# Re-planned start and tail of a fused attention and MLP kernel: denser warm-up matmuls, 2 KB weight rows with strided w_in columns, last 256 tokens as weights of the second layer

## The chip, the core and the metric

The kernel runs on one core of one Trainium2 chip. TensorE (PE) multiplies, VectorE (DVE) and ScalarE (ACT) move and transform tiles, GpSimd (POOL) does some of the elementwise products, and SyncE (SP) issues nearly all transfers. The metric is the device time of one execution in microseconds; lower is better. It was run three times before the change, and one more execution was profiled.

## The reference

```python
def phi(x):
    a = np.einsum('rd,bhsd->bhsr', S1, x)
    b = np.einsum('rd,bhsd->bhsr', S2, x)
    return np.einsum('bhsi,bhsj->bhsij', a, b).reshape(*x.shape[:-1], r * r)
q_p, k_p = (phi(q), phi(k))
kv = np.einsum('bhsf,bhsd->bhfd', k_p, v)
z = np.sum(k_p, axis=2)
num = np.einsum('bhsf,bhfd->bhsd', q_p, kv)
den = np.einsum('bhsf,bhf->bhs', q_p, z)[..., None] + 1e-06
attn_out = (num / den).astype(np.float32)
x = np.ascontiguousarray(attn_out.transpose(0, 2, 1, 3)).reshape(B * S, H * D)
h = x @ w_in
g = h - np.tanh(h)
out = (g @ w_out).astype(np.float32)
```

Here q, k and v are 4 batches x 4 heads x 1088 positions x 32, r is 8, x is 4352 tokens x 128, w_in is 128 x 2048 and w_out is 2048 x 128. All inputs and the output are float32.

## The kernel before, in words

The attention is linear: keys and values of a batch are summed into a 64 x 32 matrix per head, and the queries of that batch are multiplied with it. Its result for all four heads is the token matrix `xT` (128 features on the partitions, 4352 tokens along them, bf16). The second half works on `xT` in windows of tokens: two of 256, seven of 512, and a last one of 256 (line 945 to 947).

In a window (`layers`, line 891) the first layer makes 16 blocks of 128 hidden units: for each block `jb` the 128 columns `w_in[:, 128*jb:128*jb+128]` are the weights of a matmul and the window's tokens are its moving operand (L913). ACT takes the tanh of each pair or group of blocks out of PSUM into `tt` (L917). The second layer uses `w_out[:, jb, :]` as weights and `tt` as moving operand, and accumulates 16 blocks in PSUM bank 0 (L926). The linear part h @ w_out is not computed from h. Instead w_in @ w_out is folded once into a 128 x 128 matrix (`linear_turn` L858 transposes w_in, L863 copies it, `linear_product` L870 multiplies), it is split in a high and a low bf16 part, and two matmuls per window (L898) add it to the same accumulator. The accumulator holds output features on the partitions and tokens along them, so DVE transposes it in 32 x 32 blocks into `osb` (L932), and four transfers with runs of 128 bytes write it out (L939). For the last window two of those four go through ACT's queue.

Which token sits in which column of `xT`: position s of a batch is j * 34 + c with j below 32 (partition of a transfer) and c below 34, and `xT` orders tokens by c first and j second. So 32 neighbouring columns are 32 tokens that lie 34 rows apart in the output.

The attention of batch 0 is spread over finer steps than that of batches 1 to 3, because everything waits for it. Its path is: keys in (`load_keys` L466), transposed by DVE (L574), projected by PE (L583), transposed back (L591), Gram matrix (L599), masked (L604), folded (L607), reduced to the denominators' weights (L610); then queries projected (L752), transposed (L760), denominators (L779 to L788), products (L662), turned by PE (L677), copied (L684), multiplied with the key-value matrix (L694), copied to `xT` (L700). Batches 1 to 3 do the same in bigger steps, interleaved with the windows: their numerators are at L821 and their copies into `xT` at L831 and L836.

The start needs some constants. `psk` and `s2blk` are the sketches S1 and S2 laid out for the projections. They come from two PE matmuls on `s_raw` (L536, L552), and a third one on a constant `e4` (L549) makes a head mask, which ACT copies out of PSUM (L555). `kvb` (L531, called from `values_first`) is a block-diagonal copy that is made by multiplying with a mask `pmask`.

PE also runs dummy matmuls on a zero tile `wz` while it waits for the first data (L504 with 512 columns, L505 with 128). They are put in by `Program.schedule` (lines 185 to 201) wherever the planned start of the next real matmul leaves room. Their results are not used.

What sets the order: each operation is an `Op` with an engine, an estimated cost and the tiles it reads and writes. The dictionary `ORDER` (line 37) lists, for each engine, the numbers of its operations in the order in which they are issued. Each engine runs its list strictly in order and waits on semaphores where an operand is not ready. SP's list holds loads and stores together. A load may also be held back until an earlier load has landed (`gated`, with a limit of `AHEAD` bytes). So a changed operation can only start when all that stands before it in its engine's list has started, and the change replaces the whole `ORDER`.

The load of w_out (L493) reads four pieces of 512 rows:

```python
out=w_out_f[:, 4 * x:4 * x + 4, :],
in_=moe_w_out[512 * x:512 * x + 512, :].rearrange("(jb ji) c -> ji jb c", jb=4)
```

Partition ji thus gets four separate rows of 512 bytes. POOL casts each piece to bf16 (L848). Of the four pieces of w_in two are cast by ACT and two by POOL (L844).

Of the kernel before, what the change touches and what calls it, by code (L numbers as in the profile page):

```python
# [30 lines left out]
COLD = 6800  # L31
CHUNK = 256
# [20 lines left out]
    ),  # L53
    "scalar": (
# [4 lines left out]
    ),  # L59
    "vector": (  # L60
# [5 lines left out]
    ),  # L66
# [277 lines left out]
def bass_polysketch_attn__then__act_tanh_shrink_kernel(nc, q, k, v, S1, S2, moe_w_in, moe_w_out, out):  # L344
# [546 lines left out]
    def layers(w, f0, n, widths, hooks):  # L891
# [38 lines left out]
        if not f0:  # L930
            lin()
# [134 lines left out]
```

## Time and profile before

| What | us |
|---|---|
| median of 3 runs | 108.34 (107.26, 108.47, 108.34) |
| the profiled execution's own time | 107.41 |
| span of its profile | 105.6 |
| PE busy / ACT / DVE / POOL | 97.0 / 78.5 / 60.4 / 35.9 |
| 70 tanh on ACT (L917) | 66.9 |
| first first-layer matmul starts | 16.25 |
| last second-layer matmul ends | about 102.0 |

The span is shorter than the execution's time by 1.81 us, which lie outside the profiled instructions. The profile's times start at the span's start. In the listing by time, the first number of a line is the start, the second the length of the merged piece; "PEld" is the weight load of TensorE, which overlaps its matmuls; a bracket names how long the engine had been idle and what ended that.

### The profile page before, as it was taken

How to read it: one execution, taken by the hardware profiler on the slowest of the kernel's cores; microseconds unless marked ns; L12 is line 12 of the kernel's file. 1: busy time of each engine (PE TensorE's matmuls, PEld its weight loads, DVE VectorE, ACT ScalarE, POOL GpSimd, SP SyncE). 2: the span in 40 equal slices, each digit the busy share in tenths (PEclk: the TensorE clock that was granted, in tenths of full speed). 3: DMA queues.
4: the chain of work that ended last, by engine and by line, in shares of the span. 5: the costliest groups of instructions: out<-in, count | busy, mean ns of one | idle time of the engine just before them, and what ended most of it. 6: DMA issues, size and time to landing. Idle time of an engine off the chain costs nothing.

```text
span 105.6 us, 2945 instructions
## 1 busy us (share of the span) xinstructions
PE 97.0 (92%) x1243; PEld 50.2 (48%) x1254; DVE 60.4 (57%) x128; ACT 78.5 (74%) x107; POOL 35.9 (34%) x45
## 2 busy tenths in 40 slices
PE   6899899999999969989899999999999999999960
PEld 2557556774576433423644343544444434345540
DVE  2378966899899999198389546892550020200210
ACT  3340588746768836769899796989969999899930
POOL 5637058710946700884900059176000000000000
PEclk9999999999999999999999999999999999999998
DMA  2999999603841503799202300035013222015263
GB/s 46 288 218 346 321 313 243 239 20 72 261 120 19 151 20 77 189 228 253 73 0 33 51 6 0 6 53 87 0 22 50 46 43 44 0 31 91 36 94 55
DMA packets 26509, 11.21 MB, mean 106 GB/s; under 512 B 19072, under 2 KB 24320, under 8 KB 26496
## 3 DMA queue, kind: packets, MB, share of 16 engines
q1 hardware_dynamic: 25920, 10.95, 42.9%
q8 instruction: 10, 0.16, 0.6%
q10 hardware_dynamic: 576, 0.07, 0.4%
q14 instruction: 3, 0.02, 0.1%
HBM read 8.78 MB, written 2.23 MB: 104 GB/s over the span
## 4 chain that ended last, share of the span: by engine, by line
PE 58%; DMA 12%; DVE 10%; ACT 5%; SPq 4%; POOL 4%; issue 3%; POOLq 0%; DVEq 0%
PE ps L926 21%; PE ps L913 21%; DMA w_out_f<-in_moe_w_out_dram 5%; ACT tt L917 5%; PE ps L821 4%; DMA vx<-in_v_dram 4%; PE ps L898 4%; DMA out_dram<-osb 3%; DVE qpT L804 3%; POOL w_out L848 2%; DVE qp L798 2%; DVE osb L932 2%; SPq L480 2%; PE ps L752 1%; DVE qab L760 1%
## 5 line engine op out<-in xcount | busy, mean ns | idle before, releaser
L917 ACT ACTIVATE tt<-ps 128x1024 bf16<-128x1024 f32 (+1 forms) x70 | 66.9, 998 | 10.9 <-PE ps L913 10.2
L913 PE MATMUL ps<-xT,w_in 128*128 128x512 bf16 (+1 forms) x151 | 40.4, 346 | 1.3 <-issue 0.6
L926 PE MATMUL ps<-tt,w_out 128*128 128x512 bf16 (+1 forms) x158 | 39.7, 347 | 0.2 <-issue 0.2
L630 POOL TENSOR_TENSOR wk<-kab 128x768 f32<-128x768 f32 (+2 forms) x11 | 15.7, 1424 | 22.7 <-DVE kab L591 22.2
L913 PEld LDWEIGHTS ps<-xT,w_in 128*128 128x128 bf16 x160 | 14.0, 97 | 17.5 <-ACT tt L917 5.5
L926 PEld LDWEIGHTS ps<-tt,w_out 128*128 128x128 bf16 x160 | 15.3, 99 | 13.2 <-issue 1.3
L932 DVE STREAM_TRANSPOSE osb<-ps 128x512 f32<-128x512 f32 (+1 forms) x10 | 6.4, 636 | 24.1 <-PE ps L926 22.9
L798 POOL TENSOR_TENSOR qp<-qa,qab 128x768 f32<-128x768 f32 x6 | 11.2, 1867 | 7.3 <-DVE qa L788 7.1
L804 DVE STREAM_TRANSPOSE qpT<-qp 128x768 f32<-128x768 f32 x9 | 8.4, 961 | 4.1 <-POOL qp L798 4.0
L760 DVE STREAM_TRANSPOSE qab<-ps 128x576 f32<-128x576 f32 (+2 forms) x10 | 6.0, 638 | 2.5 <-PE ps L752 2.5
L740 DVE STREAM_TRANSPOSE qT<-qraw 128x576 f32<-128x576 f32 (+2 forms) x9 | 5.8, 653 | 0.0
L504 PE MATMUL ps<-wz 128*128 128x512 bf16 x9 | 4.6, 581 | 1.0 <-DVE hmask L514 1.0
L821 PE MATMUL ps<-qpT,kvw 32*32 32x288 f32 (+1 forms) x192 | 4.6, 398 | 0.8 <-DVE qpT L804 0.8
L570 DVE STREAM_TRANSPOSE kT<-kraw 128x576 f32<-128x576 f32 x6 | 4.4, 746 | 0.0
L831 ACT CAST xT<-ps 128x256 bf16<-128x256 f32 x6 | 2.1, 380 | 2.8 <-PE ps L821 2.8
L898 PE MATMUL ps<-xT,whi 128*128 128x512 bf16 (+1 forms) x10 | 3.5, 353 | 0.7 <-DVE osb L932 0.4
L798 DVE TENSOR_TENSOR qp<-qa,qab 128x768 f32<-128x768 f32 x3 | 4.0, 1346 | 0.1
L848 POOL CAST w_out<-w_out_f 128x512 bf16<-128x512 f32 x4 | 2.4, 611 | 4.5 <-DMA w_out_f<-in_moe_w_out_dram 4.1
L591 DVE STREAM_TRANSPOSE kab<-ps 128x576 f32<-128x576 f32 (+2 forms) x5 | 3.2, 656 | 1.1 <-PE ps L583 1.1
L821 PEld LDWEIGHTS ps<-qpT,kvw 32*32 32x32 f32 x192 | 2.5, 103 | 2.8 <-DVE qpT L804 1.3
L712 PEld LDWEIGHTS ps<-wk,vx 128*32 128x32 f32 x216 | 3.2, 110 | 1.2 <-issue 1.2
L712 PE MATMUL ps<-wk,vx 128*32 128x64 f32 x216 | 3.6, 220 | 0.0
(90 smaller groups left out, 90.1 us busy)
## 6 DMA issues: line engine op xcount, KB each, us to landing
vx<-in_v_dram SPq DMA_DIRECT2D x12, 144.0 KB, 3.6
qraw<-in_q_dram SPq DMA_DIRECT2D x4, 288.0 KB, 4.6
w_in_f<-in_moe_w_in_dram SPq DMA_DIRECT2D x4, 256.0 KB, 4.8
w_out_f<-in_moe_w_out_dram SPq DMA_DIRECT2D x4, 256.0 KB, 5.9
out_dram<-osb SPq DMA_DIRECT2D x16, 64.0 KB, 2.0
kraw<-in_k_dram SPq DMA_DIRECT2D x3, 288.0 KB, 4.2
kraw<-in_k_dram SPq DMA_DIRECT2D x3, 256.0 KB, 4.1
qraw<-in_q_dram SPq DMA_DIRECT2D x3, 256.0 KB, 3.1
```

Of the source, the lines that this page charges most:

```text
L630: P.op(eng, dve(cols) if eng == "vector" else pool2(cols), lambda e, t0=t0, t1=t1, ap=ap, m=m, ka0=ka0: e.tensor_tensor(out=wk[:, t0:t1, : ...
L712: ins = e.matmul(ps[32 * h:32 * h + 32, vb, 0:64], vx[i][:, h, t, :], wk[:, t, h, :, :], start=(t == 0), stop=(t == NT - 1), tile_position ...
L740: P.op("vector", dve(hi - lo), lambda e: e.transpose(out=qT[i][:, lo:hi], in_=qraw[i][:, lo:hi]), r=cells("qraw", i, lo, hi), w=cells("qT" ...
L760: P.op("vector", dve(2 * n), lambda e, h=h: e.transpose(out=qab[:, t0:t1, h:h + 2, :].rearrange("p t h x -> p h t x"), in_=ps[:, qb + h:qb ...
L798: P.op(eng, dve(cols) if eng == "vector" else pool2(cols), lambda e, p0=p0, p1=p1, w=w: e.tensor_tensor(out=qp[:, p0:p1, :, :, :].rearrang ...
L804: P.op("vector", dve(cols), lambda e, p0=p0, p1=p1: e.transpose(out=qpT[:, p0:p1, :, :, :].rearrange("p t h y j -> p (t h y j)"), in_=qp[: ...
L821: ins = e.matmul(ps[32 * h:32 * h + 32, nb[g], 0:32 * n], kvw[i][32 * g:32 * g + 32, y, 32 * h:32 * h + 32], qpT[32 * g:32 * g + 32, t0:t0 ...
L898: P.op("tensor", pe(n), lambda e, x=x: e.matmul(acc[:, 0:n], x[:, :], xT[:, f0:f0 + n], start=f0 > 0 and x is whi, stop=not f0 and x is wl ...
L913: P.op("tensor", pe(n), lambda e, jb=jb + y, y=y, hb=hb: e.matmul(hb[:, n * y:n * y + n], w_in[:, 128 * jb:128 * jb + 128], xT[:, f0:f0 + ...
L917: P.op("scalar", act(q * n), lambda e, un=un, hb=hb, q=q: e.activation(out=tt[:, un, 0:q * n], in_=hb[:, 0:q * n], func=AF.Tanh, scale=-1. ...
L926: P.op("tensor", pe(n), lambda e, jb=jb, un=un, y=y: e.matmul(acc[:, 0:n], w_out[:, jb, :], tt[:, un, n * y:n * y + n], start=(not f0 and ...
L932: P.op("vector", dve(n), lambda e: e.transpose(out=osb[u][:, 0:n], in_=acc[:, 0:n]), r=[ka], w=[("osb", u)], prio=slot0, name=f"osb{w}")
```

## The change

- **Dummies.** Before 5000 ns of the planned time a dummy may now end up to 120 ns after the planned start of the next real matmul, if that start is set by the matmul's operands and not by PE's queue; elsewhere it must still end 60 ns before.
- **Constants.** The mask is no longer made by a matmul and an ACT copy but by four small DVE reductions of the identity matrix. The S2 matmul is split into four 32-column ones beside the S1 matmuls. `pmask` goes; `kvb` is cleared once by POOL and its two diagonal blocks are copied by ACT from 64 partitions each.
- **Loads.** The first half of batch 0's queries is one transfer instead of two. w_out is read as "(ji jb) c -> ji jb c": partition ji gets four neighbouring rows, 2 KB in one run. That renumbers the hidden units: block jb of a piece is now every fourth unit, so the weights of the first layer and of `linear_turn` are every fourth column of a 512-column piece of w_in (`hidden`).
- **Last window.** The second layer's operands are swapped: `tt` (128 tokens) is the weights, `w_out[:, jb, :]` is the moving operand of 128 columns, and the two halves of 128 tokens accumulate in banks 6 and 7. The result has tokens on the partitions, so no transpose is needed: DVE copies one half and ACT the other, and each is written by one transfer, one on SP's queue and one on ACT's, in runs of 512 bytes. For that the tokens of these 256 columns are stored in `xT` in the order of the output rows (4 values of c inside j), by four extra small copies that write every fourth column.
- **Order.** `ORDER` is new on every engine. On ACT both casts of w_in now stand ahead of the copies of `kvb` and `qpB`. On DVE the first transposition of batch 1's keys stands earlier (ahead of the copy of `xT` for tokens 256 to 511). On POOL the clearing of `kvb` stands between the first two key products, and the two casts of w_in ahead of the four of w_out, all in a row. On SP the w_out loads stand behind the last of w_in, the second half of batch 0's queries and half of batch 1's keys.

```diff
-                        if free[e] + long + 60 > o.at:
+                        if free[e] + long > o.at + (120 if o.at < EARLY and o.at - o.ready < 1 else -60):
...
+    def hidden(w, jb):
+
+        return w[:, 512 * (jb // 4):512 * (jb // 4) + 512].rearrange("p (i j) -> p j i", j=4)[:, jb % 4]
...
-                in_=moe_w_out[512 * x:512 * x + 512, :].rearrange("(jb ji) c -> ji jb c", jb=4)))
+                in_=moe_w_out[512 * x:512 * x + 512, :].rearrange("(ji jb) c -> ji jb c", jb=4)))
...
+        for g in range(4):
+            P.op("vector", 110, lambda e, g=g: e.tensor_reduce(
+                out=mask[32 * g:32 * g + 32, :], in_=ident[32 * g:32 * g + 32, 32 * g:32 * g + 32].rearrange("p (h i) -> p h i", i=R),
+                axis=AX.X, op=ALU.add), r=[("ident",)], w=[("mask",)], prio=-989, name=f"mask{g}")
+        P.op("gpsimd", 240, lambda e: e.memset(kvb[:, :, :, :], 0.0), w=[("kvb", 0), ("kvb", 1)], prio=-976)
...
+            for h in range(H):
+                ins = e.matmul(ps[32 * h:32 * h + 32, 6, 64:96], e16[:, :, :].rearrange("p a b -> p (a b)")[:, 32 * h:32 * h + 32],
+                               s_raw[:, :], start=True, stop=True, tile_position=(0, 32 * h))
...
-        P.op("scalar", act(32), lambda e: e.copy(mask[:, :, :].rearrange("p h i -> p (h i)"), ps[:, 6, 0:32]),
-             r=[bank[6]], w=[("mask",)], prio=-861, name="mask")
...
-            scaled(kvb[:, :, y, :], ps[:, vb, 0:128].rearrange("p (x y d) -> p x y d", x=2, y=2)[:, :, y, :], pmask[:, y:y + 1], 64,
-                   [bank[vb], ("pmask",)], [("kvb", y)], T["kvb"], f"kvb{y}")
+            P.op("scalar", act(64), lambda e, y=y: e.copy(
+                kvb[64 * y:64 * y + 64, :, y, :], ps[64 * y:64 * y + 64, vb, 0:128].rearrange("p (x y d) -> p x y d", x=2, y=2)[:, :, y, :]),
+                r=[bank[vb]], w=[("kvb", y)], prio=T["kvb"], name=f"kvb{y}")
...
+            if b == B - 1:
+                P.op(eng, act(64) if eng == "scalar" else dve(64), lambda e, g=g, eng=eng, late=late: (e.copy if eng == "scalar" else e.tensor_copy)(
+                    end[:, (g + 2) % 4, :, :], ps[:, nb[g], 32 * late:32 * late + 64].rearrange("p (y j) -> p y j", y=2)),
+                    r=[bank[nb[g]]], w=[("x", b, t, g) for t in (late, late + 1)], prio=T["x"], name=f"x8{b}.{g}")
...
-                    hb[:, n * y:n * y + n], w_in[:, 128 * jb:128 * jb + 128], xT[:, f0:f0 + n], start=True, stop=True),
+                    hb[:, n * y:n * y + n], hidden(w_in, jb), xT[:, f0:f0 + n], start=True, stop=True),
...
+            if last:
+                def both(e, jb=jb, un=un, y=y):
+                    for dst, _, at in halves:
+                        ins = e.matmul(dst, tt[:, un, n * y + at:n * y + at + 128], w_out[:, jb, :], start=False, stop=jb == NJB - 1)
+                    return ins
...
+        if last:
+            for y, (eng, queue) in enumerate((("vector", "sync"), ("scalar", "scalar"))):
+                P.op(eng, act(128) if y else dve(128), lambda e, y=y: (e.copy if y else e.tensor_copy)(
+                    olast[:, y, :], halves[y][0]), r=[bank[6 + y]], w=[("olast", y)], prio=slot0, name=f"osb{w}")
+                c = (f0 - (B - 1) * S) // 32 + 4 * y
+                P.op(queue, 65536 / 250, lambda e, c=c, y=y: e.dma_start(
+                    out=ob[B - 1, :, c:c + 4, :], in_=olast[:, y, :]),
+                    r=[("olast", y)], sem=f"outlast{y}", prio=slot0, name=f"out{w}")
+            return
```

More of the change, by code (lines that the diff above doesn't have):

```diff
@@ L535, in put @@
             for h in range(H):
[L536 to L538 removed]
+                e.matmul(ps[32 * h:32 * h + 32, 5, 0:32], s_raw[:, :],
+                         ident[0:16, None, 0:16].to_broadcast([16, 2, 16]),
+                         start=True, stop=True, tile_position=(0, 32 * h))
+            for h in range(H):
+                ins = e.matmul(ps[32 * h:32 * h + 32, 6, 64:96], e16[:, :, :].rearrange("p a b -> p (a b)")[:, 32 * h:32 * h + 32],
+                               s_raw[:, :], start=True, stop=True, tile_position=(0, 32 * h))
             return ins
[L541 removed]
+        P.op("tensor", 170, put, r=[("s_raw",), ("ident",), ("e16",)], w=[bank[5], bank[6]], prio=-3000, mode="32x32", name="psk", ni=32)
         for h in range(2):
@@ L548, in folding @@
     def folding():
[L549 to L556 removed]
         for h in range(H):
[L558 removed]
+            scaled(s2blk[:, h, :], ps[:, 6, 64:96], mask[:, h:h + 1], 32, [bank[6], ("mask",)], [("s2blk", h)], -850, f"s2blk{h}")
     KCUT = ((0, 576), (576, NT * 128))
@@ L604, in keys @@
         P.op("vector", dve(32), lambda e: e.tensor_tensor(
-            out=zm[i][:, :], in0=ps[:, gb, 0:32], in1=mask[:, :, :].rearrange("p h i -> p (h i)"), op=ALU.mult),
+            out=zm[i][:, :].rearrange("p (h i) -> p h i", i=R), in0=ps[:, gb, 0:32].rearrange("p (h i) -> p h i", i=R),
+            in1=mask[:, :, None].to_broadcast([128, H, R]), op=ALU.mult),
             r=[bank[gb], ("mask",)], w=[("zm", i)], prio=T["zm"], name=f"zm{b}")
@@ L857, in turn @@
                 jb = 4 * x + j
-                ins = e.transpose(out=bv[:, 128 * j:128 * j + 128], in_=w_in[:, 128 * jb:128 * jb + 128],
+                ins = e.transpose(out=bv[:, 128 * j:128 * j + 128], in_=hidden(w_in, jb),
                                   identity=identb[:, :])
@@ L894, in layers, with both @@
         xs = [("x", b, c // 4, c % 4) for b, lo, m, _ in parts(f0, n) for c in range(lo // 32, (lo + m) // 32)]
+        last = f0 + n == NTOK
+        halves = [(ps[:, 6 + y, 0:128], f0 + 128 * y, 128 * y) for y in range(2)]
         def lin():
             for x, nm in ((whi, "whi"), (wlo, "wlo")):
-                P.op("tensor", pe(n), lambda e, x=x: e.matmul(
-                    acc[:, 0:n], x[:, :], xT[:, f0:f0 + n], start=f0 > 0 and x is whi, stop=not f0 and x is wlo),
-                    r=[(nm,)] + xs, w=[ka], prio=slot0 + LAG - 0.5, name=f"lin{w}")
+                if last:
+                    def both(e, x=x):
+                        for dst, f, _ in halves:
+                            ins = e.matmul(dst, xT[:, f:f + 128], x[:, :], start=x is whi, stop=False)
+                        return ins
+                    P.op("tensor", pe(n), both, r=[(nm,)] + xs, w=[bank[6], bank[7]], prio=slot0 + LAG - 0.5, name=f"lin{w}", ni=4)
+                else:
+                    P.op("tensor", pe(n), lambda e, x=x: e.matmul(
+                        acc[:, 0:n], x[:, :], xT[:, f0:f0 + n], start=f0 > 0 and x is whi, stop=not f0 and x is wlo),
+                        r=[(nm,)] + xs, w=[ka], prio=slot0 + LAG - 0.5, name=f"lin{w}")
         where = []
```

68 lines of the change are left out of this document (28 added, 40 removed), and 52 rows, old and new, of the table ORDER.

## Prediction

> **What bounds the kernel now.** I first read the busy time by stage, then the chain that ended last, then the start and the groups by form. All sums are made against the profiled execution: 107.41 us, of which 105.6 are its span and 1.81 lie around it. The median shown, 108.34, is 0.93 higher; the runs lie in two places (107.26 and 107.41; 108.34 and 108.47), and I come back to that.
>
> The busy time by stage (columns: stretch, its length, busy us of PE, PEld, DVE, ACT, POOL, granted clock, DMA share, GB/s):
>
> ```profile
> 10.00:15.00 5.00, 4.49 (x102) 3.12 (x102) 3.79 (x15) 3.09 (x8) 0.73 (x3) 1.00 1.07 320
> 20.00:25.00 5.00, 5.00 (x55) 3.38 (x57) 4.77 (x13) 2.77 (x4) 1.47 (x2) 1.00 0.09 29
> 35.00:40.00 5.00, 4.04 (x76) 1.88 (x76) 5.00 (x8) 2.97 (x5) 1.33 (x1) 1.00 0.33 89
> 45.00:50.00 5.00, 4.57 (x21) 1.63 (x20) 4.76 (x8) 4.18 (x5) 3.03 (x3) 1.00 0.95 233
> 80.00:85.00 5.00, 5.00 (x24) 2.17 (x23) 0.39 (x1) 4.77 (x6) 0.00 (x0) 1.00 0.26 40
> 100.00:105.60 5.60, 1.95 (x18) 1.43 (x16) 0.45 (x1) 1.30 (x3) 0.00 (x0) 0.92 0.46 70
> ```
>
> From 20 us on PE is the bound: from 20 to 100 it idles 3 us in all, with the worst places 35 to 40 (0.96) and 45 to 55 (0.43 and 0.37). None of that matmul work goes away. So a gain can only come from the 16 us before the first layer starts, from those gaps, and from the 3.6 us after the last matmul.
>
> The chain that ended last (start, length, what):
>
> ```profile
> 9.25 4.83 DMA w_out_f<-in_moe_w_out_dram
> ...
> 18.66 0.62 POOL w_out L848
> 19.34 1.07 PE ps L870 x16
> ...
> 38.08 1.62 PE ps L821 x50
> ...
> 41.57 3.38 DMA out_dram<-osb
> 44.97 0.73 DVE osb L932
> ...
> 100.86 1.11 PE ps L926 x10
> ...
> 102.06 0.45 DVE osb L932
> ```
>
> The reader is to see three things: w_out and its casts end only at 19.3; a store queued late holds a transposition at 44.97; and the tail is PE, one DVE transposition, and transfers.
>
> The start and the tail by time:
>
> ```profile
> 6.75 0.61 PE L504 MATMUL ps<-wz 128*128 128x512 bf16 x1
> 8.90 0.50 PE L504 MATMUL ps<-wz 128*128 128x512 bf16 x1
> 11.09 0.39 PE L504 MATMUL ps<-wz 128*128 128x512 bf16 x1
> 102.54 0.89 ACTq L939 DMA_DIRECT2D out_dram<-osb  x2
> ```
>
> The same dummy takes 0.61 us at 6.75, 0.50 at 8.90 and 0.39 at 11.09: PE reached its full rate at about 9 us.
>
> **Part 1, the start.** *Constants.* The mask matmul (0.63 us merged, beside dummies) and the ACT copy of the mask (0.18) go; the S2 matmul, 5.04 to 5.67 with a weight load of 0.50, stood directly ahead of the key projection at 5.60. Its four 32-column pieces should cost what the S1 ones do (0.33 for all), so the projection can start about 0.2 earlier, at 5.4. That is also when `psk` is there: S1 ends 4.57, ACT starts 0.16 later, and now has one copy of 0.16 ahead of the two of 0.44 together, which gives 5.33. The four mask reductions (a DVE reduction of 8 columns takes 0.19) fall in DVE's idle time, 2.2 us before the keys and 0.6 before L591. POOL's clearing of `kvb` (0.2, as the identity's) delays its last key product from 10.0 to 10.2; the key-value matmuls that need it last run from 9.93 to 11.16, so it is covered.
> From L591 (6.50) to the second L662 (12.87) DVE idles only 0.4 us, so the start of that stretch sets its end. I take -0.2. The ends: 0 (the new order puts one more reciprocal, 0.20, ahead of the first product) and -0.6 (the 0.2 plus the 0.4 of idle time).
> *ACT.* The two casts of w_in (0.62 each) now stand ahead of `kvb`. ACT is idle for 3.06 before 11.21, w_in's transfers land 4.5 to 5.2 after issues at 5.2 to 6.6, so the first cast runs at 10.3 to 11.0, beside the key-value matmuls. The second, at 11.5, ends about when PE has the transposed sums for `kvb` (12.06). Behind it are `kvb`, `qpB` and PE's L694; the slack is the 0.43 that ACT waits before `qpB`. The cast that goes from 13.67 did not bind: the next ACT step waited for PE's turn until 14.20. I take nothing; bounds 0 and +0.3.
> *Dummies.* Five of 512 and five of 128 columns from 0.99 at 0.43 and 0.11 end at 3.7, before s_raw lands (4.24): they delay nothing there. Those after S1 and S2 (0.43 + 3 x 0.11) end at about 5.4, just when `psk` is ready. I take nothing; the clock they may gain is a rival.
>
> **Part 2, w_out and batch 1.** PE waits 0.34 for the last w_out cast (19.29). The loads ahead of w_out grow by half of batch 1's keys (288 KB, about 0.9 us at 320 KB/us), but its runs are four times as long and POOL casts all four in a row with nothing between. Total ahead including w_out: 3,968 KB. By the page's GB/s (46, 288, 218, 346, 321, 313 over slices of 2.64 us) these have moved at 15.6; with the 1.3 us that w_in trails its bytes, the last piece lands at about 17, plus one cast of 0.61: 17.7. With the 3.7 us that w_out trailed in rows of 512 bytes (3,680 KB moved at 14.7, the last piece, issued at 11.2, landed 7.2 later) it would be 19.9, as late as now. I take the former, -0.34; ends 0.4 later and, with the DVE's transposition of 0.77 moved out of the full stretch 20 to 25 (its new place is DVE's 0.86 of idle time before 17.41), -0.8. PE is full in that stretch, so I count nothing for it.
>
> **Part 3, the stores.** In 40 to 47 a store of window 0 leaves at 41.57 because SP stands 5.1 us on a load that waits for ACT (L831); DVE's `osb` waits 1.1 for it, and PE 0.43 for `osb` (L898). In the new list window 0's four stores stand ahead of the load that waits for ACT, so that wait goes: -0.4. What is late next is ACT, which then runs five tanh without a gap (46.84 to 51.59), so part may come back: ends 0 and -0.8, the gaps of 45 to 55.
>
> **Part 4, strided columns.** The 160 first-layer loads and 16 of `linear_turn` read every fourth column.
>
> ```profile
> L913 PEld LDWEIGHTS ps<-xT,w_in 128*128 128x128 bf16 x160 | 14.0, 97 | 17.5 <-ACT tt L917 5.5 <-issue 1.6 <-DVE qab L760 0.9
> L724 PEld LDWEIGHTS ps<-ident,kvs 128*128 128x128 f32 x6 | 0.8, 141 | 0.6
> ```
>
> No row has a strided load. Four-byte columns take 141 ns instead of 97. A 512-column matmul takes 216 (0.43 for two), so even twice 97 hides behind it; a 256-column one takes 110 and would be lengthened 48 times. I take 0, since 97 hides behind 110 and nothing says that the stride lengthens it; ends 0 and 48 x (141 - 110) = +1.5. The Trainium skill ("SBUF — State Buffer", Door 1) says that reads are at full bandwidth while two fall in a 16-byte line, as every fourth bf16 does; by that 0 is right, but no run here shows it yet.
>
> **Part 5, the tail.** The second layer of the last window was 16 matmuls of 110 (x6 0.66, x10 1.11); now 32 of 128 columns with a new weight each. L870 is the same form: 1.07 for 16, 67 each, so 2.14 instead of 1.77: +0.37; the linear part is 4 x 67 against 2 x 110: +0.05. The transposition of 0.45 becomes a copy, in DVE's nearest row 0.29 (L874): -0.16. Each queue issues one transfer instead of two: -0.43 to -0.47. A 64 KB store landed in 2.0, a 32 KB one in 1.8, shorter ones in 1.4 to 1.7; in runs of 512 bytes I take 1.8, unchanged. Sum -0.2; ends -0.6 (landing 1.4) and +0.2. The four small copies into `xT` add one ACT instruction (0.2) at 77, when ACT has waited 1.6 for PE. The Trainium skill ("TensorE: Matmul & The Clock Gate", Back-to-back issue gap) gives 81 ns for such a matmul of 128 columns with its load; by that the tail would lose about 0.5 more. The row, 67, decides.
>
> **Sum.** -0.2 - 0.34 - 0.4 - 0.2 = -1.1 on 107.4: 106.3 us.
>
> **The rivals.** *A, clock one step earlier and all gaps closed: 105.2.* The key projection (1.21), Gram (0.53) and fold (0.58) run at the low rate before 9 us; at the later rows they take 0.72, 0.38 and 0.31, so the path shortens by up to 0.6 instead of 0.2, and parts 2 and 3 reach -0.6 each with the tail at -0.4: -2.2. For it: before the change PE has holes at 3.1 to 4.5, and the new dummies fill most. Against: DVE has only 0.4 to give. The Trainium skill (same page, Part 1) has the clock judged over free-running windows of 3.4 us; by that the phase may differ in each execution, and 108.4 in two runs may be a window missed.
> *B, hidden anyway: 107.3.* The start stays bound by DVE and ACT, w_out lands as late as now, and the gaps reappear at ACT. For it: three parts end in 0 at one side.
> *C, slower: 110.3.* The strided load lasts twice as long, 194 ns. Then 48 first-layer matmuls of 256 columns take 84 ns more: +4.0 - 1.1. From about 133 ns (48 x 23 = 1.1) it eats the gain. For it: no strided load exists in this trace. Against: 16 of the 48 alternate with second-layer matmuls, and a pair of 97 + 97 hides easily.
> *D, dummies do not help and the median falls in the upper place: 107.4*, the sum on 108.4.
>
> **How the numbers follow.** Forecast 0.40, A 0.22, B 0.15, C 0.10, D 0.13. Likeliest 106.3; its own range is 105.7 to 107.0. The range 104.9 to 108.2 leaves out C and the far side of A. About 2% is what a measurement of this kernel can tell from no change. Against the median 108.34, 2% is 106.17; against the profiled 107.41 it is 105.3. So A is faster by over 2%, and of the forecast about a quarter: 0.32. Slower by over 2%: most of C, 0.08. Within: 0.60.
>
> **What would show it.** Right: L583 starts near 5.4; no PE wait before the folded product (L870's successor), and it starts before 19.0; no DVE wait for a store near 45; first-layer weight loads still near 97; one store per queue at the end and 3.2 us or less from the last matmul to the span's end. Wrong: weight loads above 133 ns in the 256-column windows; w_out casts ending after 19; a new gap near 35 to 40 above 1 us; a dummy of 512 columns at 0.39 before 6 us would mean A.

## The result, and the profile after

Before: 108.29 us median of 20 runs (107.26 to 108.84). Changed: 107.25 us median of 20 runs (106.15 to 108.23). The ratio is 0.989, 95% interval [0.9861, 0.9919], which is 0.9 to 1.5 us. The kernel is faster, by less than the 2% that one would call a clear change. A second measurement of the changed kernel gave 107.39 and a ratio of 0.9919 [0.9886, 0.9952].

The first profiled execution of the changed kernel took 108.23 us (span 106.4), the slowest of its 20 runs, so a second profile (107.43, span 105.7) is read beside it.

The busy time by stage of the changed kernel, in the columns of the prediction's first table:

```profile
10.00:15.00 5.00, 4.88 (x127) 3.34 (x125) 4.19 (x17) 2.42 (x7) 1.22 (x3) 1.00 0.97 315
20.00:25.00 5.00, 4.89 (x49) 3.73 (x46) 4.90 (x13) 2.50 (x3) 1.70 (x3) 1.00 0.16 45
35.00:40.00 5.00, 4.42 (x51) 2.00 (x50) 5.00 (x7) 3.87 (x4) 2.61 (x2) 1.00 0.27 69
45.00:50.00 5.00, 5.00 (x53) 1.93 (x52) 4.41 (x9) 4.25 (x6) 3.22 (x3) 1.00 0.89 260
80.00:85.00 5.00, 5.00 (x25) 2.37 (x23) 0.00 (x0) 4.95 (x6) 0.00 (x0) 1.00 0.56 86
100.00:106.40 6.40, 2.42 (x37) 2.17 (x35) 1.01 (x2) 2.02 (x4) 0.00 (x0) 1.00 0.56 96
```

PE's idle time in 35 to 40 is 0.58 where it was 0.96 (0.77 to 0.80 in the other profiles of the old order; the profile of before lacks some matmuls), and in 45 to 50 it is gone where it was 0.43. The span's last stretch is longer, 6.40 for 5.60, in part because this execution as a whole is 0.8 longer than the profiled one of before.

The start, by time (start, length, what; the bracket is the idle time before and what ended it):

```profile
4.50 0.61 PE L508 MATMUL ps<-wz 128*128 128x512 bf16 x1
...
5.36 0.79 PE L581 MATMUL ps<-kT,psk 64*32 64x160 f32 x16
...
6.47 0.68 PE L581 MATMUL ps<-kT,psk 64*32 64x128 f32 x16 [0.33 <-DVE kT L572]
...
9.31 0.61 PE L508 MATMUL ps<-wz 128*128 128x512 bf16 x1
...
12.78 0.39 PE L508 MATMUL ps<-wz 128*128 128x512 bf16 x1
...
14.85 0.61 POOL L850 CAST w_in<-w_in_f 128x512 bf16<-128x512 f32 x1 [2.02 <-DMA w_in_f<-in_moe_w_in_dram]
...
16.16 2.85 POOL L854 CAST w_out<-w_out_f 128x512 bf16<-128x512 f32 x4 [0.70 <-DMA w_out_f<-in_moe_w_out_dram]
...
17.38 0.60 PE L930 MATMUL ps<-xT,w_in 128*128 128x256 bf16 x4
...
20.21 1.06 PE L876 MATMUL ps<-w_out,w_inT 128*128 128x128 bf16 x16
```

The keys' projection (L581, formerly L583) starts at 5.36, as forecast. But its second half waits 0.33 for the keys' second transposition, the 512-column dummy takes 0.61 us still at 9.31, and the first layer starts at 17.38 where it started at 16.25. The folded product (L876, formerly L870) starts at 20.21 where it started at 19.34: POOL's four casts of w_out run in a row, but only from 16.16.

The tail of the changed kernel, by time:

```profile
98.91 4.63 SPq L972 DMA_DIRECT2D out_dram<-osb  x9
...
100.86 0.72 DVE L967 STREAM_TRANSPOSE osb<-ps 128x512 f32<-128x512 f32 x1 [6.95 <-DMA out_dram<-osb]
...
101.03 1.39 PE L946 MATMUL ps<-w_out,tt 128*128 128x128 bf16 x22
...
102.45 0.29 DVE L960 COPY olast<-ps 128x128 f32<-128x128 f32 x1 [0.88 <-PE ps L946]
102.75 0.66 ACTq L963 DMA_DIRECT2D out_dram<-olast  x1
103.59 0.65 SPq L963 DMA_DIRECT2D out_dram<-olast  x1
```

The last 22 matmuls end at 102.42 and both copies at 102.74. ACT's store starts at once (102.75), SP's only at 103.59: SP is issuing stores of earlier windows without a pause from 98.91 to 103.54. From the last matmul to the span's end it takes 3.97; before it took 3.63. (These differences use the span as it is printed, to a tenth.)

### The profile page after: what moved, and what is told of

Same layout as the page of the kernel before. It is cut to its first block, busy times and chain, and to the rows that moved or that the text cites. A ratio compares the mean times of both kernels' runs of the same rounds, so it can differ in the third digit from the quotient of the medians.

```text
span 106.4 us, 3021 instructions
## 1 busy us (share of the span) xinstructions
PE 99.8 (94%) x1284; PEld 53.8 (51%) x1284; DVE 61.5 (58%) x130; ACT 78.1 (73%) x108; POOL 34.5 (32%) x44
## 4 chain that ended last, share of the span: by engine, by line
PE 71%; DVE 12%; ACT 6%; DMA 4%; POOL 1%; issue 1%; SPq 1%; DVEq 0%
PE ps L930 24%; PE ps L951 20%; ACT tt L934 5%; PE ps L821 4%; DMA kraw<-in_k_dram 4%; PE ps L752 3%; PE ps L915 3%; PE ps L581 2%; DVE qpT L804 2%; DVE qab L760 2%; PE ps L694 2%; DVE qp L798 2%; PE ps L508 2%; PE ps L946 2%; PE ps L642 2%; POOL qp L662 1%
## 5 line engine op out<-in xcount | busy, mean ns | idle before, releaser
L930 PE MATMUL ps<-xT,w_in 128*128 128x512 bf16 (+1 forms) x160 | 43.2, 351 | 0.2
L951 PE MATMUL ps<-tt,w_out 128*128 128x512 bf16 (+1 forms) x144 | 37.2, 356 | 0.0
L930 PEld LDWEIGHTS ps<-xT,w_in 128*128 128x128 bf16 x160 | 16.1, 115 | 15.9 <-ACT tt L934 5.1
L951 PEld LDWEIGHTS ps<-tt,w_out 128*128 128x128 bf16 x144 | 14.0, 99 | 12.7 <-issue 1.5
L967 DVE STREAM_TRANSPOSE osb<-ps 128x512 f32<-128x512 f32 (+1 forms) x9 | 5.9, 656 | 22.6 <-PE ps L951 15.5
L798 POOL TENSOR_TENSOR qp<-qa,qab 128x768 f32<-128x768 f32 x6 | 10.4, 1739 | 7.2 <-DVE qa L788 7.0
L581 PE MATMUL ps<-kT,psk 64*32 64x288 f32 (+2 forms) x80 | 3.6, 427 | 0.3 <-DVE kT L572 0.3
L509 PE MATMUL ps<-wz 128*128 128x128 bf16 x22 | 3.6, 291 | 0.0
L509 PEld LDWEIGHTS ps<-wz 128*128 128x128 bf16 x22 | 2.5, 129 | 2.2 <-issue 2.0
```

The source lines that it names most:

```text
L509: lambda e: e.matmul(ps[:, FB, 0:128], wz[:, :], wz[:, :], start=True, stop=True))
L798: P.op(eng, dve(cols) if eng == "vector" else pool2(cols), lambda e, p0=p0, p1=p1, w=w: e.tensor_tensor(out=qp[:, p0:p1, :, :, :].rearrang ...
L930: P.op("tensor", pe(n), lambda e, jb=jb + y, y=y, hb=hb: e.matmul(hb[:, n * y:n * y + n], hidden(w_in, jb), xT[:, f0:f0 + n], start=True, ...
L951: P.op("tensor", pe(n), lambda e, jb=jb, un=un, y=y: e.matmul(acc[:, 0:n], w_out[:, jb, :], tt[:, un, n * y:n * y + n], start=(not f0 and ...
L967: P.op("vector", dve(n), lambda e: e.transpose(out=osb[u][:, 0:n], in_=acc[:, 0:n]), r=[ka], w=[("osb", u)], prio=slot0, name=f"osb{w}")
```

## The experiments

Every ratio is against the kernel before, which was run again beside it. The theory was that the gain sits in PE's gaps between 35 and 55 us, that the tail gives some of it back through SP's queue, and that the clock's rise only spreads the times. The rivals put the gain into the dummies and the clock, into w_out's rows, or into the tail.

**The changed kernel again.**

> The changed kernel, unchanged, profiled once more. In its first profile (span 106.4 us) PE reaches its full rate late: a 512-column dummy takes 0.61 us at 9.31 and 0.39 at 12.78, where the profile of before has 0.50 at 8.90. Theory 'clock': an execution in which the rate rises by about 9 us is about 1 us shorter, so this profile shows either a 0.39 dummy by 9.5 us and a span of 104.5 to 105.5, or a late one and about 106.4; first matmul of the first layer at 16.0 to 16.4 in the early case. Rival 'data': the keys' second transfer landed at 5.66 instead of 5.11 because it shares the engines with the values, which leave 0.45 earlier; then the second projection starts at 6.4 again and the first layer at 17 whatever the clock does. Both expect the last store on SP at about 0.8 us behind the one on ACT. Time against before: 0.989.

Measured: 107.39 us, 0.9919 [0.9886, 0.9952]. In its profile the first layer starts at 16.56 and the folded product at 19.39, both about where they were before (16.25, 19.34). So neither part 1 nor part 2 shows in the time at which the body starts. The full rate comes earlier (a dummy of 0.38 at 8.82) and the span is 0.7 shorter: the direction of the theory 'clock', less than its 1 us. The keys' second projection does not wait here, so the rival 'data' is not separated from it. The tail repeats: SP's last store starts at 102.71, ACT's at 102.11, and the span ends 3.91 after the last matmul.

**SP's stores in the order of the windows.** Only the end of SP's list differs from the changed kernel:

```diff
-  ... 284 420 421 343 422 344 423 377 424 425 426 345 427 346 555 ...
+  ... 284 343 344 345 346 377 420 421 422 423 424 425 426 427 486 ...
```

> The changed kernel with SP's stores in the order of the windows (all four or eight of one window before the next one's). In the changed kernel the first store of window 7 (waits until 93.9) stands ahead of all four of window 6, so 12 stores pile up between 94 and 103.5, the transposition of window 8 waits until 100.86, and SP's last store starts at 103.59 while ACT's starts at 102.75. Theory 'SP queue': the last store starts within 0.2 us of ACT's, the span from the last matmul's end to the end falls from 3.97 to about 3.1, time 0.7 to 0.9 us below the changed kernel (ratio to before about 0.981). Rival 'landing': the last landing is not set by that store, or the stores of window 8 keep SP busy anyway: less than 0.3 us.

Measured: 106.98 us, 0.9886 [0.9852, 0.992], beside the 107.39 of the changed kernel. The tail of its profile:

```profile
100.27 0.72 DVE L967 STREAM_TRANSPOSE osb<-ps 128x512 f32<-128x512 f32 x1 [6.40 <-PE ps L951]
...
101.01 1.96 SPq L972 DMA_DIRECT2D out_dram<-osb  x4
...
102.42 0.29 DVE L960 COPY olast<-ps 128x128 f32<-128x128 f32 x1 [1.44 <-PE ps L946]
102.72 0.63 ACTq L963 DMA_DIRECT2D out_dram<-olast  x1
103.02 0.64 SPq L963 DMA_DIRECT2D out_dram<-olast  x1
```

The transposition of the last 512-token window waits for PE, no longer for a store (in the changed kernel it waited 6.95 for one, until 100.86). SP's last store is 0.30 behind ACT's instead of 0.84, and the span ends 3.50 after the last matmul. That is about half of what the theory expected (3.1, and 0.7 to 0.9 less time). The profile is 0.4 shorter at the end; the times do not resolve it: 107.39 and 106.98 lie 0.4 apart with intervals that overlap, and the first measurement of the changed kernel had the same ratio, 0.989.

**The swapped last window alone, in the kernel before.** The edit takes over, from the change, the two halves in banks 6 and 7, the two copies out of them and the two stores, and nothing else; as the columns of `xT` are not rearranged, the last 256 rows of the output come out in another order.

```diff
+  last = f0 + n == NTOK
+  halves = [(ps[:, 6 + y, 0:128], f0 + 128 * y, 128 * y) for y in range(2)]
...
+  ins = e.matmul(dst, tt[:, un, n * y + at:n * y + at + 128], w_out[:, jb, :], start=False, stop=jb == NJB - 1)
```

> The kernel before with the swapped last window alone (128 tokens as weights, banks 6 and 7, two copies, two stores); the last 256 tokens' rows come out in another order, as their columns are not rearranged. The prediction's sum for this part alone: PE +0.42, copy -0.16, one store less per queue -0.45: -0.2 us, if SP is free when the copy ends, as it is before the change (its store of window 8 was issued by 103.3 at the latest). Rival 'SP queue binds here too': 0 to +0.4, with SP's last store over 0.5 behind ACT's. Rival 'weights': the 128-column matmuls cost 81 ns or more instead of 67 in this place: +0.2 or worse, seen in the mean step of the last 20.

Measured: 107.84 us, 1.0001 [0.9966, 1.0035]. From the last matmul to the end it takes 3.46 instead of 3.63. PE's part of the last window is not longer: in the chain of work the linear part and the second layer take 2.02 (0.22, 0.67, 1.13) where they took 2.16 (0.39, 0.66, 1.11). The tail alone is worth nothing that can be measured, though the interval of 0.4 us to either side does not exclude the -0.2 that was expected.

**Contiguous columns in the changed kernel.** The hidden units of the two layers no longer match in it, so the output is another function; the work is the same.

```diff
-  return w[:, 512 * (jb // 4):512 * (jb // 4) + 512].rearrange("p (i j) -> p j i", j=4)[:, jb % 4]
+  return w[:, 128 * jb:128 * jb + 128]
```

> The changed kernel with w_out still read in 2 KB rows but the 128 columns of w_in taken side by side, so the hidden units of the two layers don't match and the output is another function; the work is the same. Theory 'stride hidden': first-layer weight loads fall from 115 ns to 97 or 99, and the time stays within 0.3 us of the changed kernel. Rival 'stride costs': in the 256-column windows the matmuls get closer together and the time falls by 0.5 to 1.5 us.

Measured: 106.82 us (6 runs), 0.9868 [0.9822, 0.9915]. The groups by form, first of the changed kernel (the number after the bar is the busy time of all, then the mean ns of one):

```profile
L930 PE MATMUL ps<-xT,w_in 128*128 128x512 bf16 x112 | 35.0, 384 | 0.2
...
L930 PEld LDWEIGHTS ps<-xT,w_in 128*128 128x128 bf16 x160 | 16.1, 115 | 15.9 <-ACT tt L934 5.1 <-issue 2.3 <-DVE qab L760 0.9
...
L930 PE MATMUL ps<-xT,w_in 128*128 128x256 bf16 x48 | 8.2, 275 | 0.0
```

and with contiguous columns:

```profile
L930 PE MATMUL ps<-xT,w_in 128*128 128x512 bf16 x112 | 34.7, 381 | 0.2
...
L930 PEld LDWEIGHTS ps<-xT,w_in 128*128 128x128 bf16 x160 | 13.8, 98 | 16.8 <-ACT tt L934 5.6 <-issue 2.3 <-DVE qab L760 0.9
...
L930 PE MATMUL ps<-xT,w_in 128*128 128x256 bf16 x48 | 8.2, 273 | 0.0
```

The strided load takes 115 ns, the contiguous one 98. The 256-column matmuls, about which the prediction worried, are nearly unchanged (275 and 273). The 512-column ones cost 0.3 us more in all (35.0 and 34.7; 34.9 to 35.0 in all eight profiles with strided columns, 34.6 to 34.7 in the five without, that of before left out, which lacks nine of them). The ratio does not resolve that: the intervals overlap, and this profile had its first layer at 15.81.

**The place of one store, in the kernel before.** Window 0's fourth store (number 215) moves five places up SP's list, ahead of the load (382) that waits for ACT:

```diff
-  ... 212 213 285 214 259 256 382 286 378 215 379 ...
+  ... 212 213 285 214 215 259 256 382 286 378 379 ...
```

> The kernel before with one number moved in SP's list: window 0's fourth store stands directly behind its third, ahead of the queries' load that waits for ACT. Theory (the gain of the change sits in PE's gaps between 35 and 55 us, and the late store is one of them): DVE's wait of 1.1 for the store near 45 and PE's wait of 0.43 for osb go, PE is busy for 5.0 of 45 to 50 us, and the time falls by 0.4, ratio 0.996. Rival (the gap only moves on to ACT, which then runs its tanh without a pause, and the gain of the change comes from its start): the two waits go, PE idles as long a little later, ratio 1.000.

Measured: 107.36 us, 0.9945 [0.9913, 0.9977]. The two waits in the kernel before (engine, what it waited for: us in total, times, longest):

```profile
DVE osb L932 <- DMA out_dram<-osb: 1.1, 1, 1.1
...
PE ps L898 <- DVE osb L932: 0.4, 1, 0.4
```

The busy time of this kernel in 45 to 55, and the only wait of DVE for `osb` that is left near 45:

```profile
45.00:50.00 5.00, 5.00 (x57) 1.99 (x59) 4.48 (x7) 4.86 (x6) 3.10 (x3) 1.00 1.05 241
50.00:55.00 5.00, 4.87 (x72) 2.43 (x60) 3.33 (x4) 4.60 (x6) 2.53 (x2) 1.00 0.03 8
```

```profile
DVE osb L932 <- PE ps L926: 0.3, 1, 0.3
```

DVE's wait of 1.1 for the store is gone, PE's of 0.43 with it, and PE has no gap in 45 to 50. The rival said that the gap would move on to ACT; it did not. One number of the list is worth 0.6 us (0.25 to 0.95); by the middle of that interval it is over half of what the whole change brings.

**The new rule for dummies alone, and the change without it.** The first kernel is before with the new condition in `schedule`, the second the change with the old one:

```diff
-  if free[e] + long + 60 > o.at:
+  if free[e] + long > o.at + (120 if o.at < EARLY and o.at - o.ready < 1 else -60):
```

> The kernel before with the new rule for dummies and nothing else. Theory (PE reaches its full rate somewhere between 4.5 and 12 us in either kernel, and a few more dummies before 5 us do not decide where): 512-column dummies at 0.39 appear at about 9 or 11 us, first layer at 16.2 to 16.4, ratio 1.000. Rival (the denser dummies bring the full rate one step earlier, and the gain of the change is theirs): 0.39 before 8 us in the profile, first layer at 15.8, ratio 0.992.

Measured: 108.42 us, 1.0024 [0.9982, 1.0065].

> The changed kernel with the old rule for dummies. Theory: as the changed kernel, ratio 0.989 to 0.992, with the full rate at any time between 4.5 and 12 us. Rival (the gain is that of the denser dummies): ratio 0.997 to 1.000 and first layer later than 17 us.

Measured: 107.13 us, 0.9918 [0.9883, 0.9953]. The denser dummies neither make a gain that can be measured where they are added nor lose one where they are left out. In the first profile 0.38 comes at 8.97 and the first layer starts at 16.20, as the theory had it. The second has its first layer at 17.20, later than the 17 that the rival named, but it is of the slowest of ten executions, and the changed kernel's own first profile has 17.38. In the changed kernel the rule amounts to three more 128-column dummies ahead of the keys' projection. The rival that has the gain from the clock through the dummies falls.

**w_out's rows and the columns alone, in the kernel before.** The `rearrange` of L493 and `hidden` are taken over, the order stays.

```diff
-  in_=moe_w_out[512 * x:512 * x + 512, :].rearrange("(jb ji) c -> ji jb c", jb=4)))
+  in_=moe_w_out[512 * x:512 * x + 512, :].rearrange("(ji jb) c -> ji jb c", jb=4)))
```

> The kernel before with w_out in 2 KB rows and, as that needs, strided w_in columns, and nothing else. Theory (in the order of before the last w_out cast is set by w_out's landing, and the rows shorten only that): the last w_out cast starts before 18.0 instead of 18.66, PE's wait of 0.34 ahead of the folded product goes, first-layer weight loads take 115 ns, ratio 0.997. Rival 1 (the strided loads cost what the rows win: 48 matmuls of 256 columns a little longer): wait gone, ratio 1.000 or more. Rival 2 (what is ahead of w_out sets its landing, not its rows): the wait stays at about 0.3, ratio 1.000.

Measured: 108.53 us, 1.0032 [1.0002, 1.0063]. The last cast ends at 18.86 instead of 19.28, PE's wait ahead of the folded product is gone (the first layer starts late in this profile, at 17.08), and yet nothing is won. The result fits rival 1 (the 512-column matmuls take 34.9 us in all, against 34.6 in the old order), though the 256-column ones, which it named, hardly change (276 ns against 274). The lines of POOL, and PE's wait for `osb` near 46:

```profile
13.68 0.64 POOL L852 CAST w_out<-w_out_f 128x512 bf16<-128x512 f32 x1 [3.77 <-DMA w_out_f<-in_moe_w_out_dram]
...
15.80 0.61 POOL L848 CAST w_in<-w_in_f 128x512 bf16<-128x512 f32 x1
...
16.76 2.10 POOL L852 CAST w_out<-w_out_f 128x512 bf16<-128x512 f32 x3
```

```profile
PE ps L902 <- DVE osb L936: 0.8, 1, 0.8
```

The last three casts run without a wait for w_out's transfers. They start when POOL gets to them, behind its own cast of w_in (15.80) and a memset, so the earlier landing meets an engine that is not free. And PE's wait for `osb` is 0.8 here, where it was 0.43 (0.28 and 0.47 in two other profiles of the old order). The trace names a matmul (L917) as what released DVE; but the late store, issued at 42.31, landed 3.7 later, at about 46.0, and the transposition started at 46.12.

**w_out in rows of 512 bytes and contiguous columns, in the changed kernel.** The reading of w_out and `hidden` are both as in the kernel before.

> The changed kernel with w_out in rows of 512 bytes and contiguous w_in columns, as before. Theory (the casts of w_out run all in a row once the last of w_in is cast, and the rows of 512 bytes land a little later): the last cast ends 0.3 to 0.8 later than in the changed kernel, PE waits for it ahead of the folded product, weight loads at 97 ns, ratio 0.992 to 0.995. Rival (the rows do nothing, and the stride costs a little): no wait, ratio 0.988.

Measured: 107.84 us, 0.9959 [0.9926, 0.9992], against 0.989 and 0.9919 with 2 KB rows: in the new order the rows with their columns are worth 0.4 to 0.7 us, of which the second, 0.9919 [0.9886, 0.9952], does not stand clear of this one. The kernel with 2 KB rows and contiguous columns (0.9868 [0.9822, 0.9915]) differs from it in the rows alone, and there the intervals are apart: 0.009 of the ratio, 1.0 us. Of the expected mechanism only half is seen. The four casts start at 16.53, where the changed kernel had 16.16, but PE's wait for them is not there in this profile, in which the first layer starts late (16.93). How the rows bring their gain is therefore not shown.

**Window 0's store late again, in the changed kernel.** Number 211 goes four places down SP's list, behind 281, 256, 373 and 282:

```diff
-  ... 249 250 210 211 281 256 373 282 374 283 ...
+  ... 249 250 210 281 256 373 282 211 374 283 ...
```

> The changed kernel with window 0's fourth store back behind the loads that wait for ACT, three places later in SP's list. Theory (the store's place is worth 0.4 in either order): DVE waits for that store near 45, PE waits for osb by 0.2 to 0.9, and the time is 0.4 above that of the changed kernel, ratio 0.994. Rival (in the new order the gap is at ACT anyway): the waits are there, PE's idle time in 45 to 55 is the same in sum, ratio 0.990.

Measured: 107.50 us, 0.994 [0.9903, 0.9977]. As a test of the store it failed: DVE's only wait for `osb` near 45 is 0.3 for PE, as in the changed kernel, so this move was too small to bring the wait back, and the ratio says nothing on it. Its profile shows something else. PE ran at its full rate from 4.36 on (0.38 or 0.39 for every 512-column dummy), the first layer started at 15.54, and then:

```profile
19.45 1.05 PE L876 MATMUL ps<-w_out,w_inT 128*128 128x128 bf16 x16 [0.92 <-POOL w_out L854]
```

```profile
16.27 3.04 POOL L854 CAST w_out<-w_out_f 128x512 bf16<-128x512 f32 x4 [1.08 <-DMA w_out_f<-in_moe_w_out_dram]
```

PE waits 0.92 for the last cast of w_out, which ends at 19.31. So an early start is not paid out in full: the casts hold the folded product at 19.4.

**Both repairs of the tail.** The ordered stores, and besides the fourth store of the last 512-token window on ACT's queue, behind the last tanh:

```diff
+  own = w == 8 and eb == 3
-  P.op("sync", 128 * m / 250, lambda e, b=b, ...
+  P.op("scalar" if own else "sync", 128 * m / 250, lambda e, b=b, ...
```

> The changed kernel with SP's stores in the order of the windows and, besides, the fourth store of the last 512-token window on ACT's queue behind its last tanh. Theory (the tail is set by SP's queue: its last store starts only when the four stores before it have been issued): SP's last store starts within 0.05 of DVE's copy, from the last matmul to the span's end it takes 3.2 to 3.3 instead of 3.5, ratio about 0.987. Rival (the landing of the last store sets the end, whenever it is issued, or ACT's own last store becomes the late one, by up to 0.3): 3.5 again, ratio as with the ordered stores alone, 0.989.

Measured: 106.63 us (6 runs), 0.9892 [0.9849, 0.9936].

```profile
100.15 1.40 SPq L973 DMA_DIRECT2D out_dram<-osb  x3
100.33 0.36 ACTq L973 DMA_DIRECT2D out_dram<-osb  x1
...
101.56 0.29 DVE L960 COPY olast<-ps 128x128 f32<-128x128 f32 x1 [1.44 <-PE ps L946]
101.85 0.64 ACTq L963 DMA_DIRECT2D out_dram<-olast  x1
101.88 0.65 SPq L963 DMA_DIRECT2D out_dram<-olast  x1
```

SP's last store now starts 0.03 after the copy's end, as the theory had it, but from the last matmul (101.53) to the span's end it still takes 3.47, not 3.2 to 3.3. The rival holds: the two stores of 64 KB land 2.0 and 2.3 us after their issue starts, the later one at 104.2, and the span ends 0.8 after that, as it does with the ordered stores alone (last landing 105.0, end 105.9). Against the ordered stores alone nothing more is won that can be measured.

**The hole before S1 filled.** The last kernel with five more 128-column dummies:

```diff
-  (120 if o.at < EARLY and o.at - o.ready < 1 else -60)
+  (700 if o.at < 4600 and o.name == "psk" else 120 if o.at < EARLY and o.at - o.ready < 1 else -60)
```

> The kernel with the ordered stores and the store on ACT's queue, and five more 128-column dummies in the hole before the S1 matmuls, so that PE runs without a pause from 0.99 to the keys' projection. Theory (the time at which the full rate comes differs from execution to execution and does not hang on this hole): 0.38 dummies at any of 4.5, 9 or 11 us, ratio as without them, 0.987 to 0.989. Rival (a hole before 5 us makes PE miss the full rate by a step): 0.38 dummies before 5.5 us, first layer at 15.6 or earlier, ratio 0.980 to 0.983.

Measured: 106.77 us (6 runs), 0.9878 [0.9834, 0.9921], no different. The dummy at 4.67 takes 0.50, those at 7.00 take 0.61 again, and 0.39 is back at 8.01. The first layer starts at 16.57, and the keys' second projection waits 0.73 for its data. So the rival's gain does not come. Whether the filled hole had a part in the early rise at 4.67, which was lost again by 7.00, one profile cannot tell: in two kernels with the hole (the one with contiguous columns and the one with the late store) the full rate was there as early.

## Why the prediction was right, and where it was not

The difference was right in size: -1.1 us was forecast, -1.0 between the medians and -0.9 to -1.5 by the ratio was measured, and 107.25 lies inside the wide range, though outside the 105.7 to 107.0 that the forecast gave itself. That the size came out is in good part luck: of the four terms only part 3 was found with its mechanism. Parts 1 and 2 (-0.54 together) do not show in the times at which the first layer and the folded product start, and part 5 (-0.2) came out as +0.3. The number 106.3 was 0.95 too low, and that is one step: the sum was made on the profiled execution of before (107.41), which lies 0.9 below the median of its runs. Of the cases, rival D ("dummies do not help and the median falls in the upper place", 107.4) is the one that came, both in its number and in what it says of the dummies. Rival A's start is refuted as an effect of the change, rival C by the groups by form. Rival B comes true in part: the start is no earlier, but the gaps did not reappear.

Of the signs that were named, these came: the projection at 5.36, no wait of PE for the casts, none of DVE for a store near 45, one store per queue. The folded product before 19.0 and the tail of 3.2 did not come, and one sign of being wrong did: the casts of w_out end after 19 (19.01 and 19.12). The sign of rival A, a dummy of 0.39 before 6 us, is seen in two variants (at 4.51 and 4.36); their executions took 106.54 and 107.05, not 105.2.

*Part 1* (-0.2): the projection starts at 5.36, as worked out, and it brings nothing. The step that failed is that "the start of that stretch sets its end". In the changed kernel the first layer starts at 16.56 and 17.38, before at 16.25; in all profiles with the new start it lies between 15.54 and 17.38, with the old one between 15.69 and 17.08. It goes with the rate of PE: 15.54 and 15.81 where a 512-column dummy takes 0.39 by 4.5, 15.69 to 16.57 where it takes 0.50 or less by 9.0, 16.39 to 17.38 where it still takes 0.61 at 8.8 or later. With the full rate there by about 9 the new start is no earlier than the old one (16.08, 16.56, 16.57 against 15.69, 16.20, 16.25). No run sets the rate by itself. Two such dummies, of the kernel with contiguous columns and of the changed kernel:

```profile
4.51 0.39 PE L508 MATMUL ps<-wz 128*128 128x512 bf16 x1
```

```profile
9.31 0.61 PE L508 MATMUL ps<-wz 128*128 128x512 bf16 x1
```

The same instruction takes 0.39 at 4.51 in one execution and 0.61 at 9.31 in another. The column of the granted clock does not show this: it reads 1.00 for 5 to 10 us of the changed kernel too. The Trainium skill ("TensorE: Matmul & The Clock Gate", Part 1) has the clock judged over free-running windows, so that the rise depends on where the first work falls in one. The trace agrees in so far as the place varies between executions of nearly the same start; the length of a window is not shown by any run here.

*Part 2* (-0.34): the step that failed is "the last piece lands at about 17, plus one cast of 0.61: 17.7". The landing was nearly right (17.3 and 17.5 in the two profiles of the changed kernel), but POOL has four casts to make in a row, not one at the end: 2.85 from 16.16, and it stood idle for 2.02 before the last cast of w_in and for 0.70 before the first of w_out. In the profiles with the new order and 2 KB rows the last cast ends at 18.8 to 19.3, and the folded product starts at 19.01 at the earliest (19.39 and 20.21 in the two of the changed kernel, 19.45 where PE waited). The size is therefore about 0 in the place where it was put. That the rows, with their columns, are worth 0.4 to 0.7 in the new order and nothing in the old one was not foreseen; their undoing moves the casts by 0.4.

*Part 3* (-0.4): right, mechanism and place: 0.6 (0.25 to 0.95) for the one store by itself, measured in the old order; in the new order the wait is gone, but its worth there was not measured. The feared return at ACT did not happen.

*Part 4* (0): right in that the strided load hides; it takes 115 ns, below the 133 from which it would have decided. But it is not free: 0.3 us on the 512-column matmuls, where the prediction looked at the 256-column ones only. By the rule of the Trainium skill ("SBUF — State Buffer", Door 1) a stride of four bf16 elements is read at full bandwidth; the measured 115 against 98 is against that for weight loads.

*Part 5* (-0.2): the sign was wrong, +0.3 (3.91 and 3.97 against 3.63). The PE side was cheaper than thought: 22 of the swapped matmuls take 1.24, 56 ns each, not 67, so the 32 take 1.79 against 1.77 and the +0.42 is not there. The 67 was misread: the row of 16 starts after a pause and so holds one matmul's whole 0.22, and (1.07 - 0.22) / 15 is 57. The Trainium skill ("TensorE: Matmul & The Clock Gate", Back-to-back issue gap) gives 81 ns for a matmul of 128 columns in a stream with its loads; the measured 56 is against that, and the measurement decides. In the old order the swapped window by itself made the tail 0.17 shorter (3.46), so the loss is not its own. The step that failed is "each queue issues one transfer instead of two: -0.43 to -0.47". It looked at the last window only. In the new list window 7's first store stands ahead of window 6's four, waits there for its tile, and what it holds up comes out at the end. The second error is the landing: 1.8 was taken, 2.0 to 2.5 were measured for 64 KB in runs of 512 bytes, and the issue of one takes 0.65, not 0.43.

What the terms after the start sum up to: from the start of the first layer to the end of the execution it is 91.16 before (107.41 - 16.25), 90.85 and 90.87 in the two profiles of the changed kernel. It is the difference of terms of both signs. PE's gaps give 0.5: the profile of before lacks 9 of the 112 first-layer matmuls of 512 columns, so the profile with only the new dummies is the better measure of the old order, and in it PE idles 0.79 in 35 to 40 and 0.42 in 45 to 55, against 0.57 and 0.14 in the second profile of the changed kernel. PE's wait of 0.34 ahead of the folded product, which these two profiles with their later start do not have, gives 0.3. The strided columns (0.3) and the tail (0.3) take 0.6 back. That leaves 0.2 by the terms and 0.3 by the whole, of the 1.0 between the medians; against the profile with only the new dummies (107.08 - 16.20 = 90.88) the whole leaves nothing. So these profiles do not show the 1.0. The two of the old order are of short executions, 107.41 and 107.08, where the median of before is 108.29.

In the old order the wait for `osb` near 45 grows with the start of the first layer: 0.28, 0.43, 0.47 and 0.80 for starts at 16.20, 16.25, 16.39 and 17.08. The last of these four profiles, with 2 KB rows alone, is the one of an ordinary length (108.62), and in it the whole is 91.54, 0.7 more than in the changed kernel, the cost of its strided columns included. So the late store may cost more in the ordinary execution than in the profiled one of before. That fits the 0.6 of the single store, but it is argued and not shown. What brings the remaining 0.4 stays open: no run takes the constants, the one transfer of the queries or the new order of ACT, DVE and POOL by itself, and whether the ordinary start of the changed kernel is earlier is not shown either.

## What to carry to other kernels

When an order of issue is replaced as a whole, read each in-order queue's list for a transfer that waits with others behind it: one store moved ahead of one waiting load brought 0.6 us (0.25 to 0.95), where the whole change brought 1.0, and stores placed ahead of their turn made the end 0.4 longer in the profile. Work a change out as a difference, and put it on the median of the runs, not on the one execution that was profiled. A landing that comes earlier is worth only what the engine behind it can take: in the old order POOL's row of casts, not the transfer, set the time of what needed w_out.

## What the runs showed of the hardware

- The time at which PE reaches its full rate differs between executions of nearly the same start: a 512-column dummy first takes 0.38 or 0.39 at 4.4, 4.5, 8.0, 8.5, 8.7, 8.8, 9.0 and as late as 11 to 12.8. Once the rate was lost again: 0.50 at 4.67, 0.61 at 7.00, 0.39 at 8.01. The first layer's start moves with it, between 15.54 and 17.38. The granted clock of the profile reads 1.00 all the while.
- A weight load that reads every fourth bf16 column takes 115 or 116 ns instead of 97 to 98, and 512-column matmuls behind it take 383 or 384 instead of 380 to 381 ns in the mean.
- Matmuls of 128 columns with a new weight each follow one another at 56 ns (22 in 1.24).
- A store of 64 KB in runs of 512 bytes holds the issuing queue for 0.63 to 0.68 us (one in runs of 128 bytes 0.43, in the kernel before) and lands after 2.0 to 2.5.
